# GpSimd waits on a semaphore for VectorE's operation at their shared port, and a planner with other lags orders the kernel

## The chip, the cores and the metric

The kernel runs on one core of one Trainium2 chip. The metric is the device time of one execution in microseconds: 879.89 us for the kernel before, the median of three runs (879.86 to 881.14). The engines are TensorE (PE; PEld is its weight loading), VectorE (DVE), ScalarE (ACT), GpSimd (POOL) and SyncE (SP), whose queue starts nearly all DMA transfers.

## The reference

Three blocks follow one another. Inputs are float32; the weights of the two feed-forward blocks are float64 in the kernel's arrays and are turned into float32 on the chip when they come so.

```python
# attention: 4 batches, 8 heads, 576 positions, 64 per head
scores = q @ k.T / 8
scores = where(scores >= max(scores) - tau, scores, -1e9)
a = exp(scores - max(scores)); a = a / (sum(a) + 1e-9)
x = (a @ v).transpose(0, 2, 1, 3).reshape(2304, 512)
# first feed-forward block, 512 -> 1024 -> 512, with SoLU and a layer norm
h = x @ w_in
s = h * softmax(h)
x = ((s - mean(s)) / sqrt(var(s) + 1e-6) * g_ln) @ w_out
# second feed-forward block, 512 -> 2048 -> 512, with Mish
h = x @ w2_in
out = (h * tanh(log1p(exp(h)))) @ w2_out
```

## The kernel before

The kernel is written as a list of tasks, and a planner puts them in order. Each task names its engine, a duration, the tasks whose results it reads (`deps`), the buffers it takes and those it uses. `Plan.run` (L344) builds the order once with a list scheduler (`forward`, L258) and then issues every task in that order, so each engine's instruction stream is fixed by it. At each step the scheduler picks, for every engine, the ready task with the best rank, and the rank is mainly the task's key: three characters of the table `KEYS` (L19) for each task. A lag is added between a task and one that reads its result (`lag`, L218); a change of TensorE between forms of matmul costs `DRAIN` (L201). Tasks marked `port` (all of GpSimd's, and VectorE's operations that use the port which the two engines share) are planned one after the other. That order at the port is only planned: on the chip each engine starts a task when its own operands are there.

The work has three stages that overlap.

- Attention, to about 410 us. Per pair of heads and block of 128 rows: scores on TensorE (L729 as four-pass float32 products, L737 as products of words split in two), the row maximum on VectorE (L743), the exponential on ScalarE (L744), the threshold on GpSimd (L746, one column), mask and row sum on VectorE (L747), transposes on TensorE (L774 to L779), their copies on ScalarE (L755), and the product with the values (L824). The score tile `st` has two buffers, so L747 on one tile lets a later score product start.
- First feed-forward block, tokens in tiles of 128, from about 30 to 530 us: products with `w_in` (L881), SoLU and layer norm on ScalarE, VectorE and GpSimd (L897 to L911), transposes (L930), products with `w_out` (L951). Float64 weights arrive by DMA and are converted by VectorE (L579 to L587) and GpSimd (L590, L593); each is split into a high and a low word (ScalarE L604, GpSimd L605).
- Second feed-forward block, from about 450 us to the end. Its two products are done with seven block products in place of eight; the sums and differences that this needs are VectorE's and GpSimd's (L640, L969, L1100, L1107, L1171). A product (`product`, L1042) is three matmuls for each chunk of 128: high word by high, low by high, high by low. `ff_in` makes the hidden layer and applies Mish (ScalarE L1103), then splits it into `gh` (L1133) and `gl` (L1135). `ff_out` loads the weight chunk `B7`, splits it (ScalarE L1074, VectorE L1076), and each of its products covers two chunks g of the hidden layer.

In the names, `hoa` and `hob` are the accumulator banks of the last stage, `m` the small tile of row maximum and threshold, `e` the exponentials, `cz` and `cf` the steps of the weight conversion, `ws` the converted weight.

Of the kernel before, what the change touches and what calls it, by code (L numbers as in the profile page):

```python
# [19 lines left out]
    "gb3a+veLPbt8VvljZ9ZCqiUCdfTaZGZm5cfqijBdYnnJga95YPFfc7bC3cXhh1EXXefoyiCrax8X/1g0xb+Dg95dl9a93ifsexPfeQZhedzbcSjf5rcZXeUD"  # L20
    "aoYfREaygewPfUAclGhh7dJ/amSdxtglrdIBcDdbIfdddhDtau3dZibbRV8ecg7bEoirveP3cVbotjX1Wc4UeczdAOhQNexJcubdh/crCZ3MdvWcJJiGnesS"
    "eZvcsXffda3kfMQd3eefOcRWd2ccYJcJ2b9wgMCcNQfkYd5DcwSgYubUFhZBWTfaKDbjnbKGax7dNZat4hppbM8erBes8fZLd3/bgYd1veAxeJpeiheTWdhm"
    "eg6gyvacUfvRcSkdNFawta4DcXMc2gePEhQ6cxUdgDdHVdlkdyBe9zgH4dgXWzxclmcBMdj6cWSdppa/7b3+arAZarYWNesOdInbakZzdd0Fcr4XezV70bkY"
    "XxJayWZcwexWYYyYwkVwPYAIcX5ce4cG/kUtZ4zbc1Yu9d2maukgmxbG9YVNbgEXUTbGnZz/dhydoqclGWoYYoPZcbYmuW41bbpXJXX9WYfAYr6X0Kb89Wu9"
    "cBZWo5ZBdW3GZitY4WacqYWEYfaYmKYSGdxPcVQaqnXi2YGSYZKYIyYtHZw1XsxYAfY0pW9ZUjNZR4XUNXsWXqYZNJedAX2hYIyXl2YfrXqqXuqYTvW61Wo6"
    "ZOxYEGWS1ZRJhzYXlsakAYnDWXjYEfXTfZETWGHbSiXoUX0sTeaZCfXiQXhjXLrWJoYA2YgBW5+aZ1YfPVYrYCIWoBaYjYfnV3hXr1XyrWoKVKBa8MW7fWM9"
    "YnTVilWG5XQmYFZTv3Y8MVEfZ4JXnIW8uWd/Vt3VoiaqMXi2WK8XjlVUJYOaTmhWwGVricBCYZyZnFXxhXmKWEgWanWMST60XRyXZ8ZuoaFMX2+YeuaLqV9p"
    "VokUsoWCPabhXihYfbYLnYc2TdrZCIeEsYkYVmIZDuYdcbIpZF0XiBcUqbvaaOBXOQTTaUKOYgMbyjYoiXb1XTYWSlZXlaZhWZwWt7c4WVKxa+9TP+RtlT1T"
    "WeUZirWRRaBhY+EYdJakSYrBY53bctMfEXldTyMULNYTFSTubTjZkKUqITyBaXdZdpZeIXJWWgVVapT9NS9NWwPTwkYylUAzT4vYV0WEbYTeWxLUH8aAvSef"
    "Za4U9jSVgVYCY4qYV1WP/UxQcb5QbsUjfTycVrGaPFZpbTlPT8qVAkZqvRyhVZ8X2YV8kXD9U1oVXUS5JT/lXdZVC4UCjYiUY4MX3KWDHYvIZk/TIJSqtUg6"  # L30
    "SEVTBVUG5UP+SYtYH3aaYWHjSBwTR3SfMX7JVdoTY5XTVTl5Vf7UPFTilP4vYmuRLNWvjW4wTu/UyLT7ORbPUdvVhBSq+UedRUqU5WSiUTS/VGyWb6VlTTG2"
# [360 lines left out]
def kernel(  # L392
# [30 lines left out]
    CW = 512  # L423
# [839 lines left out]
```

## Time and profile before

| | us |
|---|---|
| median of three runs | 879.89 (879.86 to 881.14) |
| the profiled execution | 878.76 |
| its span, first to last instruction | 876.7 |
| TensorE busy | 850.4 (97%) |
| VectorE busy | 764.1 (87%) |
| ScalarE busy | 614.6 (70%) |
| GpSimd busy | 327.3 (37%) |

The times of single instructions below come from the profiled execution. Matmuls are pipelined and their ends are modelled: a busy TensorE can still be slower than its pace, which is read from the number of matmuls in a stretch. An operation on VectorE or GpSimd that has to wait for the shared port does so inside its own duration, so a long maximum beside a short median is such a wait.

### The profile page before, as it was taken

The page shows a single profiled execution, that of the slowest core. Times are in us where ns is not written, and L with a number is a line of the kernel's source. Part 1 is how long each engine was busy: PE and PEld are TensorE (multiplying, and loading weights), DVE is VectorE, ACT ScalarE, POOL GpSimd, SP SyncE. Part 2 cuts the span into 40 slices and gives each one's busy share as a digit, 9 for nine tenths or more (in the row PEclk, how much of TensorE's full clock was granted, in tenths as well). Part 3 has the DMA queues.
Part 4 walks back from the last instruction along what each step waited for, and adds up shares of the span by engine and source line. Part 5 has one row for each costly group of instructions (what it writes and reads, how often), then busy time and mean ns, then how long its engine had stood idle before and what let it go on. Part 6 is the DMA issues. An engine that isn't in the chain of part 4 may idle for free. (4 is left out here: it accounts for less than half of the span.)

```text
span 876.7 us, 16504 instructions
## 1 busy us (share of the span) xinstructions
PE 850.4 (97%) x5423; PEld 736.1 (84%) x5423; DVE 764.1 (87%) x1638; ACT 614.6 (70%) x1292; POOL 327.3 (37%) x370
## 2 busy tenths in 40 slices
PE   8999999999999999999999999999999999999998
PEld 4556666787787978888888898999999899999998
DVE  6988899889899989999865898998899999878796
ACT  5898988878788878787654776765766555656461
POOL 2677766556675647444222321111122202010000
PEclk8999999999999999999999999999999999999999
DMA  6665444336736384454799499999899869887641
GB/s 225 184 215 190 148 137 144 104 96 201 223 122 186 121 261 156 134 189 132 245 396 306 162 285 310 343 348 332 292 298 336 272 223 307 305 285 252 211 160 72
DMA packets 155573, 195.22 MB, mean 223 GB/s; under 512 B 15312, under 2 KB 112608, under 8 KB 155488
## 3 DMA queue, kind: packets, MB, share of 16 engines
q1 hardware_dynamic: 155344, 194.17, 68.4%
q8 instruction: 43, 0.70, 0.3%
q14 instruction: 42, 0.34, 0.1%
q10 hardware_dynamic: 144, 0.00, 0.0%
HBM read 142.94 MB, written 51.19 MB: 221 GB/s over the span
## 5 line engine op out<-in xcount | busy, mean ns | idle before, releaser
L1047 PE MATMUL hoa<-gh,B 128*128 128x384 f32 x488 | 124.2, 335 | 0.6 <-DVE acc L1171 0.6
L747 DVE SCALAR_TENSOR_TENSOR e<-st,m,e 128x576 f32<-128x576 f32 x139 | 111.4, 813 | 14.9 <-ACT e L744 10.5
L1047 PE MATMUL hoa<-y,A 128*128 128x384 f32 x594 | 117.9, 337 | 3.1 <-ACT gf L1097 2.1
L744 ACT ACTIVATE e<-st,m 128x576 f32<-128x576 f32 x139 | 101.2, 742 | 23.9 <-DVE m L743 23.3
L1107 POOL TENSOR_TENSOR gf<-gf 128x384 f32<-128x384 f32 x24 | 30.7, 1280 | 224.2 <-DVE gf L1107 212.0
L743 DVE TENSOR_REDUCE m<-st 128x1 f32<-128x576 f32 x139 | 102.2, 751 | 11.8 <-PE st L729 6.4
L1047 PEld LDWEIGHTS hoa<-y,A 128*128 128x128 f32 x594 | 103.0, 188 | 6.2 <-ACT gf L1097 3.5
L1133 ACT ACTIVATE gh<-gf 128x384 fp32r<-128x384 f32 x168 | 81.9, 519 | 27.5 <-DVE gf L1107 15.3
L1135 DVE TENSOR_TENSOR gl<-gf,gh 128x384 fp32r<-128x384 f32 x168 | 90.0, 573 | 0.7 <-PE hob L1047 0.7
L774 PE MATMUL p_ta<-ident,e 128*128 128x128 f32 x576 | 84.9, 280 | 4.2 <-ACT ex L755 1.0
L1047 PEld LDWEIGHTS hoa<-gh,B 128*128 128x128 f32 x488 | 87.8, 188 | 1.4 <-DVE acc L1171 1.1
L746 POOL TENSOR_SCALAR m<-m,cs 128x1 f32<-128x1 f32 x144 | 55.6, 388 | 87.1 <-DVE m L743 68.6
L774 PEld LDWEIGHTS p_ta<-ident,e 128*128 128x128 f32 x576 | 66.1, 142 | 24.5 <-ACT ex L755 4.6
L590 POOL TENSOR_TENSOR ws<-cf,cl 128x512 uint32<-128x512 uint32 x32 | 47.0, 1470 | 100.0 <-DMA w2c<-ws 38.3
L951 PE MATMUL p_mo<-LH,W2H 128*128 128x256 f32 x288 | 83.9, 291 | 0.4 <-DVE LL L936 0.4
L951 PE MATMUL p_mo<-LL,W2H 128*128 128x256 f32 x288 | 81.6, 283 | 0.1
L1047 PE MATMUL hoa<-gl,B 128*128 128x384 f32 x244 | 81.6, 334 | 0.0
L951 PE MATMUL p_mo<-LH,W2L 128*128 128x256 f32 x288 | 81.3, 282 | 0.0
L1103 ACT ACTIVATE gf<-gf 128x384 f32<-128x384 f32 x72 | 37.4, 522 | 42.8 <-DVE gf L1100 42.3
L1171 DVE TENSOR_TENSOR acc<-acc,hoa 128x384 f32<-128x384 f32 x106 | 57.0, 548 | 10.8 <-PE hoa L1047 9.6
L881 PE MATMUL p_mo<-W1H,XH 128*128 128x512 f32 x144 | 60.9, 423 | 0.7 <-DVE ln L903 0.6
L729 PE MATMUL st<-Kst,Qhh 64*128 64x320 f32 (+1 forms) x300 | 52.6, 441 | 4.3 <-DVE e L747 2.8
(127 smaller groups left out, 2245.0 us busy)
## 6 DMA issues: line engine op xcount, KB each, us to landing
A<-w2c SPq DMA_DIRECT2D x140, 256.0 KB
y<-yc SPq DMA_DIRECT2D x28, 768.0 KB
w2c<-ws SPq DMA_DIRECT2D x32, 448.0 KB
B<-w2c SPq DMA_DIRECT2D x112, 128.0 KB
cr<-w_in SPq DMA_DIRECT2D x32, 256.0 KB
cr<-w_out SPq DMA_DIRECT2D x32, 256.0 KB
yc<-yh SPq DMA_DIRECT2D x9, 896.0 KB
yc<-ys SPq DMA_DIRECT2D x9, 896.0 KB
```

The costliest lines, as they stand in the source:

```text
L729: TE.matmul(flat()[:, c:c + w], f(qh.tile[a, i * 128:(i + 1) * 128]), f(ks.tile[a, k:k + w]), start=(y == 0), stop=(y == len(heads) - 1))
L743: t = add("DVE", dve(S), lambda: V.tensor_reduce(m.tile[:, 2:3], x(), AX.XY, ALU.max, negate=True), [t], [m], [st])
L744: a = add("ACT", act(S, True) + 0.1, lambda: SC.activation(et(), x(), ACTF.Exp, bias=m.tile[:, 2:3]), [t], [e] if h == 0 else (), [st, m, ...
L746: b = add("POOL", 0.26, lambda: G.tensor_scalar(m.tile[:, 1:2], m.tile[:, 2:3], -1.0, nt8, ALU.mult, ALU.add), [t], use=[m])
L747: t = add("DVE", dve(S) + 0.06, lambda: V.scalar_tensor_tensor(et(), x(), m.tile[:, 1:2], et(), ALU.is_ge, ALU.mult, accum_out=sr.tile[:, ...
L774: TE.transpose(tp.tile[:, k * 128:(k + 1) * 128], e.tile[:, o:o + 128], ident)
L881: TE.matmul(h.tile, l.tile[:, kt], r[:, kt, j * 512:(j + 1) * 512], start=(kt == 0 and x == 0), stop=(kt == KD - 1 and x == 2))
L951: TE.matmul(y.tile[:, :PN], l[:, k, cs], r.tile[:, k], start=(k == 0 and x == 0), stop=(k == KF - 1 and x == 2))
L1047: TE.matmul(x.tile[:, :TH], l, r, start=new and n == 0, stop=stop and n == len(steps) - 1, skip_group_check=True)
L1133: a = add("ACT", act(TH), lambda h=h, x=x: SC.activation(h.tile, full(x), ACTF.Copy), [first], [h], [h, x])
L1135: out[c] = h, l, add(e, cost(TH), lambda h=h, l=l, x=x, eng=eng: eng.tensor_tensor(l.tile, full(x), f(h.tile), ALU.subtract), [a, *deps], ...
L1171: d = add("DVE", dve(TH), lambda: V.tensor_tensor(to(), to(), fr(), ALU.add), deps + [CO.get((v, e, i, t))], use=[ac, x])
```

## The change

Five things change, and with them the order of nearly every engine.

1. After every VectorE task that uses the shared port, the next GpSimd task gets a semaphore wait on it (`add_manual_dep` in `run`). The planner adds 0.2 us (`HAND`) between the two. VectorE's small sum L767 now counts as a user of the port.
2. The lags of the planner are a table by pair of engines (`LAG`), and the cost of a change of form on TensorE is a table (`CHANGE`) in place of 0.24.
3. An operand can be marked `Late`: the planner lets the task start although this operand comes some matmuls later. Tasks with high and low words name each word by itself.
4. `product` takes its terms in turns: with two chunks, one matmul of the first, one of the second, and so on.
5. The table of keys is another, so the order is; some durations in the plan are others.

The diff, cut to its core. Of the 127 lines of the table, before and after, the first stands for all.

```diff
 KEYS = (
-    "gb3a+veLPbt8VvljZ9ZCqiUCdfTaZGZm5cfqijBdYnnJga95YPFfc7bC3cXhh1EXXefoyiCrax8X/1g0xb+Dg95dl9a93ifsexPfeQZhedzbcSjf5rcZXeUD"
+    "io3bPeVUwaR9hdbeQVcd1hnVXPUdbHiNem8zcYDa4yca/gXgczbegzfFuaSHgQ3Y+8d3Fdl8bYnqPtfD0fHfZhWd7Rd51f+9icwYSEhLPfg2dxjb4rfZ0e+3"
...
+class Late:
+    def __init__(self, task, after):
+        self.task, self.after = task, after
...
-    DRAIN = 0.24
+    CHANGE = (0.0, 0.19, 0.135), (0.186, 0.0, 0.1), (0.1, 0.12, 0.0)
+    HAND = 0.2
+    LAG = {"PE": {"ACT": 0.205, "DVE": 0.195}, "ACT": {"ACT": 0.135, "DVE": 0.155, "POOL": 0.19, "PE": 0.165},
+           "DVE": {"DVE": 0.12, "ACT": 0.12, "POOL": 0.2, "PE": 0.16}, "POOL": {"POOL": 0.14, "DVE": 0.1, "PE": 0.12}}
...
     def lag(d, t):
-        if d == t:
-            return 0.0 if t in ("PE", "-") else 0.13
-        return 0.0 if d == "SP" else 0.2 if d == "PE" else 0.27 if t == "PE" else 0.16
+        if d == "SP" or d == t and t in ("PE", "-"):
+            return 0.0
+        return Plan.LAG.get(d, {}).get(t, 0.2 if d == "PE" else 0.16)
...
                     if t.mode != mode:
-                        at = max(at, now + self.DRAIN)
+                        at = max(at, now + self.CHANGE[mode][t.mode])
                 elif t.port:
-                    at = max(at, port)
+                    at = max(at, port, hand if e == "POOL" else 0.0)
...
             if t.port:
                 port = t.end
+                if t.eng == "DVE":
+                    hand = t.end + self.HAND
...
-            t.lags = [(d, self.lag(d.eng, t.eng) if data else None) for d, data in t.need]
+            t.lags = [(d, None if z is None else self.lag(d.eng, t.eng) - z) for d, z in t.need]
...
+            made = self.tc.nc.cur_bb.bb.instructions
+            n = len(made)
             t.fn()
+            if t.port:
+                if t.eng == "DVE":
+                    last = made[-1]
+                elif last is not None:
+                    self.tc.add_manual_dep(made[n], last.name, SYNC, reason="shared port")
+                    last = None
...
-            d = add("DVE", 0.08, lambda: V.tensor_scalar(sums(), sums(), 1.0e-9, None, ALU.add), RX[p][1:], use=[sr])
-            deps = deps + [add("DVE", 0.13, lambda: V.reciprocal(sums(), sums()), [d], use=[sr])]
+            d = add("DVE", 0.08, lambda: V.tensor_scalar(sums(), sums(), 1.0e-9, None, ALU.add), RX[p][1:], use=[sr], port=True)
+            deps = deps + [Late(add("DVE", 0.13, lambda: V.reciprocal(sums(), sums()), [d], use=[sr]), 0.1)]
...
-            steps = [(l, r) for a, b in terms for l, r in zip(a(), b())]
+            steps = [x for y in zip(*(zip(a(), b()) for a, b in terms)) for x in y]
...
-            return product(1, terms, x, new, [Bs[c, g][1] for g in gs] + [GC[v, g][c][2] for g in gs] + deps,
+            return product(1, terms, x, new, [x for n, g in enumerate(gs) for x in (Late(Bs[c, g][1], n * one), Late(Bs[c, g][2], (2 + n) * one), Late(GC[v, g][c][2], n * one), Late(GC[v, g][c][3], (4 + n) * one))] + deps,
```

The products with `w_in` and `w_out` and the value product get `Late` or separate operands in the same manner.

The order of VectorE's instructions at the start of attention, before. `m` is a row maximum, `e` the masked exponentials of the score tile named behind it, `cz` a step of a weight's conversion; L743 to L769 are the same operations under the line numbers of either kernel.

```order
L743 TENSOR_REDUCE m_214<-st_203 128x1
L743 TENSOR_REDUCE m_220<-st_211 128x1
L743 TENSOR_REDUCE m_227<-s3_217 128x1
L747 SCALAR_TENSOR_TENSOR e_222,sr_233<-st_203,m_214,e_222 128x576
L747 SCALAR_TENSOR_TENSOR e_222,sr_233<-st_211,m_220,e_222 128x576
L584 TENSOR_SCALAR cz_241<-cz_241 128x512
L743 TENSOR_REDUCE m_257<-st_243 128x1
L747 SCALAR_TENSOR_TENSOR e_246,sr_233<-s3_217,m_227,e_246 128x576
```

The same place after the change:

```order
L765 TENSOR_REDUCE m_210<-st_202 128x1
L765 TENSOR_REDUCE m_222<-st_212 128x1
L769 SCALAR_TENSOR_TENSOR e_217,sr_226<-st_202,m_210,e_217 128x576
L765 TENSOR_REDUCE m_235<-s3_207 128x1
L769 SCALAR_TENSOR_TENSOR e_217,sr_226<-st_212,m_222,e_217 128x576
L765 TENSOR_REDUCE m_255<-st_237 128x1
L769 SCALAR_TENSOR_TENSOR e_242,sr_226<-s3_207,m_235,e_242 128x576
L765 TENSOR_REDUCE m_268<-st_261 128x1
```

The masked product on the first score tile stands third instead of fourth, and the conversion step is no longer among the first two pairs of tiles.

TensorE's first product of `ff_out`, before: `gh` and `gl` are the high and low half of the hidden layer, `B7` the weight chunk, with a high and a low word, and the bracket names the engine that is waited for.

```order
L1047 MATMUL hob1_7021<-gh_6525,B7_6941 128x384 [waits Activation_49]
L1047 MATMUL hob1_7021<-gh_6525,B7_6941 128x384 [waits DVE_49]
L1047 MATMUL hob1_7021<-gl_6737,B7_6941 128x384
L1047 MATMUL hob1_7021<-gh_6875,B7_6952 128x384 [waits Activation_49]
L1047 MATMUL hob1_7021<-gh_6875,B7_6952 128x384 [waits DVE_49]
L1047 MATMUL hob1_7021<-gl_6987,B7_6952 128x384
```

The same product after the change:

```order
L1070 MATMUL hob1_7003<-gh_6495,B7_6914 128x384
L1070 MATMUL hob1_7003<-gh_6830,B7_6923 128x384
L1070 MATMUL hob1_7003<-gh_6495,B7_6914 128x384 [waits DVE_49]
L1070 MATMUL hob1_7003<-gh_6830,B7_6923 128x384
L1070 MATMUL hob1_7003<-gl_6732,B7_6914 128x384
L1070 MATMUL hob1_7003<-gl_6963,B7_6923 128x384
```

The two chunks alternate; the word that VectorE makes is waited for at the third matmul, where it was the second, and the low half comes fifth and sixth.

GpSimd's stream from the first conversion of a weight to the making of its low word `W1L`, before; `xo` is the attention's output tile, `Qhh` and `Q2` are scaled queries.

```order
L593 TENSOR_TENSOR cf_313<-cf_313,cl_236 128x512 [waits Activation_49]
L689 TENSOR_SCALAR Qhh_262<-Qhh_262,cs_130 128x256 [waits DMAHW2_49,PE_49]
L746 TENSOR_SCALAR m_340<-m_340,cs_130 128x1 [waits DVE_49,Activation_49,Pool_49]
L699 TENSOR_SCALAR Q2_238<-Q2_238,cs_130 128x640 [waits DMAHW0_49]
L746 TENSOR_SCALAR m_357<-m_357,cs_130 128x1 [waits DVE_49,Activation_49,Pool_49]
L689 TENSOR_SCALAR Qhh_327<-Qhh_327,cs_130 128x256 [waits DMAHW5_49,PE_49]
L843 TENSOR_TENSOR xo_332<-xo_332,rx_306 128x256 [waits DMAHW1_49,DMAHW0_49,Activation_49]
L746 TENSOR_SCALAR m_405<-m_405,cs_130 128x1 [waits DVE_49,Pool_49]
L746 TENSOR_SCALAR m_377<-m_377,cs_130 128x1
L689 TENSOR_SCALAR Qhh_371<-Qhh_371,cs_130 128x256 [waits DMAHW3_49,PE_49]
L746 TENSOR_SCALAR m_417<-m_417,cs_130 128x1 [waits DVE_49,Pool_49]
L605 TENSOR_TENSOR W1L_132<-cf_313,W1H_131 128x512 [waits Activation_49]
```

The same stretch after the change:

```order
L615 TENSOR_TENSOR cf_303<-cf_303,cl_311 128x512 [waits Activation_49]
L768 TENSOR_SCALAR m_368<-m_368,cs_130 128x1 [waits DVE_49,Pool_49]
L711 TENSOR_SCALAR Qhh_333<-Qhh_333,cs_130 128x256 [waits DMAHW6_49,PE_49]
L865 TENSOR_TENSOR xo_324<-xo_324,rx_308 128x256 [waits DMAHW7_49,DMAHW0_49,Activation_49]
L627 TENSOR_TENSOR W1L_132<-cf_303,W1H_131 128x512 [waits DVE_49,Activation_49]
L768 TENSOR_SCALAR m_402<-m_402,cs_130 128x1 [waits DVE_49]
L768 TENSOR_SCALAR m_408<-m_408,cs_130 128x1 [waits DVE_49]
L711 TENSOR_SCALAR Qhh_377<-Qhh_377,cs_130 128x256 [waits DMAHW3_49,PE_49]
```

The low word has a wait on VectorE that it did not have, and three operations stand between the conversion and it, where there were ten.

## Rows read from the trace of the kernel before

**Rows 1.** Busy time by stage: span, PE, PEld, DVE, ACT, POOL (instructions); clock, DMA share, GB/s.

```profile
0.00:18.80 18.80, 14.75 (x62) 8.24 (x62) 11.79 (x31) 9.59 (x17) 2.70 (x13) 0.82 0.67 219
18.80:154.00 135.20, 128.80 (x842) 82.72 (x842) 119.78 (x256) 118.11 (x240) 96.82 (x130) 1.00 0.56 172
154.00:308.00 154.00, 150.82 (x1091) 124.27 (x1091) 138.84 (x294) 126.38 (x259) 93.42 (x112) 1.00 0.49 151
308.00:528.00 220.00, 216.28 (x1505) 187.79 (x1504) 185.66 (x402) 157.31 (x307) 85.07 (x83) 1.00 0.71 227
528.00:704.00 176.00, 171.75 (x974) 167.71 (x973) 163.55 (x352) 114.52 (x268) 32.61 (x22) 1.00 0.95 316
704.00:872.90 168.90, 168.00 (x959) 165.38 (x957) 143.98 (x305) 88.73 (x204) 16.63 (x13) 1.00 0.68 227
872.90:876.70 3.80, 0.01 (x1) 0.00 (x0) 0.56 (x1) 0.00 (x0) 0.00 (x0) 0.77 0.37 145
sum 876.70, PE 850.41 PEld 736.11 DVE 764.15 ACT 614.64 POOL 327.26; mean PE 121.49 PEld 105.16 DVE 109.16 ACT 87.81 POOL 46.75
```

**Rows 2.** Waits on TensorE: engine, line waited for, us in total, times, longest.

```profile
PE st L729 <- DVE e L747: 2.8, 4, 1.9
PE hoa L1047 <- ACT gf L1097: 2.1, 3, 1.6
```

**Rows 3.** Busy time in two full stretches of the last stage; columns as above.

```profile
792.00:814.00 22.00, 22.00 (x128) 21.83 (x128) 19.30 (x41) 13.41 (x32) 1.19 (x1) 1.00 0.76 249
814.00:836.00 22.00, 22.00 (x129) 22.00 (x128) 15.95 (x32) 10.57 (x22) 2.40 (x2) 1.00 0.71 226
```

**Rows 4.** All engines in order of time at the start: start, us, instruction, [idle before].

```profile
1.19 4.18 PE L527 MATMUL p_ta<-warm 128*128 128x512 bf16 x11 [1.19 <-DVE warm L524]
...
1.66 1.37 SPq L687 DMA_DIRECT2D Qhh<-qq  x3
...
6.00 0.35 DVE L689 TENSOR_SCALAR Qhh<-Qhh,cs 128x256 f32<-128x256 f32 x1 [1.33 <-DMA Qhh<-qq]
...
7.27 0.76 DVE L743 TENSOR_REDUCE m<-st 128x1 f32<-128x576 f32 x1 [0.25 <-PE st L729]
...
7.94 0.75 DVE L743 TENSOR_REDUCE m<-s 128x1 f32<-128x576 f32 x1
...
8.61 0.81 DVE L747 SCALAR_TENSOR_TENSOR e<-st,m,e 128x576 f32<-128x576 f32 x1
...
9.57 0.77 PE L729 MATMUL st<-Kst,Qhh 64*128 64x320 f32 x4 [1.92 <-DVE e L747]
...
11.30 0.43 DVE L584 TENSOR_SCALAR cz<-cz 128x512 f32<-128x512 f32 x1 [1.14 <-ACT cz L582]
...
11.64 0.75 DVE L743 TENSOR_REDUCE m<-st 128x1 f32<-128x576 f32 x1
```

**Rows 5.** All engines in order of time, entry to the second feed-forward block.

```profile
528.65 0.43 DVE L579 TENSOR_SCALAR cz<-cr 128x512 uint32<-128x512 uint32 x1 [1.54 <-DMA cr<-w_in]
...
531.93 0.53 ACT L1103 ACTIVATE gf<-gf 128x384 f32<-128x384 f32 x1 [3.00 <-DVE gf L1100]
...
534.24 1.32 PE L1047 MATMUL hoa<-y,A 128*128 128x384 f32 x6 [1.56 <-ACT gf L1097]
...
536.24 0.44 PE L1047 MATMUL hob<-gh,B 128*128 128x384 f32 x1 [0.50 <-DVE B L1076]
```

**Rows 6.** Port users by line: count, duration ns min/median/max, first and last start us.

```profile
L640 DVE TENSOR_TENSOR ws<-ws x128: 227/285/1653, 178.4 to 731.4; 128x128 f32<-128x128 f32 x128
...
L579 DVE TENSOR_SCALAR cz<-cr x32: 412/428/1793, 162.2 to 723.3; 128x512 uint32<-128x512 uint32 x32
...
L746 POOL TENSOR_SCALAR m<-m,cs x144: 255/266/1321, 7.1 to 406.4; 128x1 f32<-128x1 f32 x144
```

**Rows 7.** TensorE in order of time at two changes between forms of matmul.

```profile
60.36 0.81 PE L729 MATMUL st<-Kst,Qhh 64*128 64x256 f32 x4 [0.16 <-PE p_ta L824]
...
88.78 0.81 PE L729 MATMUL st<-Kst,Qhh 64*128 64x256 f32 x4 [0.22 <-issue]
```

More of the change, by code (lines that the diff above doesn't have):

```diff
@@ L209, in add @@
         t.new = list(new)
-        t.need = [(d, True) for d in deps if d is not None] + [(d, False) for d in order if d is not None]
+        t.need = [(d.task, d.after) if isinstance(d, Late) else (d, 0.0) for d in deps if d is not None]
+        t.need += [(d, None) for d in order if d is not None]
         for x in t.new:
@@ L292, in put @@
         def put(b, t, open_, stale):
-            nonlocal port, dma, table, mode
+            nonlocal port, hand, dma, table, mode
             t.begin, t.end = b, b + t.dur
@@ L364, in run @@
                 if x.k:
[L365 removed]
+                    t.need.append((b.slots[x.k - 1].taker, None))
                 if b not in self.rings:
@@ L574, in convert @@
             hw = lambda: cr.tile[:, :, 1]
-            t2 = add("ACT", act(CW), lambda: SC.activation(cl.tile, cr.tile[:, :, 0], ACTF.Copy, scale=2.0 ** -29),
+            t2 = add("ACT", 0.56, lambda: SC.activation(cl.tile, cr.tile[:, :, 0], ACTF.Copy, scale=2.0 ** -29),
                      t_f, [cl], [cr])
@@ L581, in convert @@
             else:
-                t1 = add("ACT", act(CW), lambda: SC.activation(f(cz.tile), f(hw()), ACTF.Abs), t_f, [cz], [cr], table="exp")
+                t1 = add("ACT", 0.56, lambda: SC.activation(f(cz.tile), f(hw()), ACTF.Abs), t_f, [cz], [cr], table="exp")
             t3 = chain("DVE", [
@@ L832, in pv @@
         for ks in (range(0, 2), range(2, KT), range(KT, QT)):
-            t = add("PE", pe(len(ks), w, 4) + 0.015, lambda ks=ks: go(ks), [d for y in [*x, u] for d in y[1:]] + [vt] if t is None else [],
+            t = add("PE", pe(len(ks), w, 4) + 0.015, lambda ks=ks: go(ks), [d for y in x for d in y[1:]] + [vt] if t is None else u[1:] if KT in ks else [],
                     [acc] + [xo] * (not xo.taker) if t is None else (), [acc, v] + slots, order=[t or xo.taker], mode=2)
-        EVT[p].append(add("ACT", act(w, True) + 0.05, lambda: SC.activation(xo.tile[:, cs], acc.tile[:, :w], ACTF.Copy),
+        EVT[p].append(add("ACT", act(w, True), lambda: SC.activation(xo.tile[:, cs], acc.tile[:, :w], ACTF.Copy),
                           [t], (), [acc, xo]))
@@ L876, in moe_h @@
         so, (xh, xl) = SO[t][0], XSL[t]
-        h, last_t = b_two.new(), None
+        h, last_t, one = b_two.new(), None, pe(1, 512)
         def go(kt):
@@ L884, in moe_h @@
         for kt in range(KD):
-            last_t = add("PE", pe(3, 512) + 0.02, lambda kt=kt: go(kt), XSP[t] + [W1T[kt, c] for c in range(j * 512, j * 512 + 512, CW)],
+            last_t = add("PE", pe(3, 512) + 0.02, lambda kt=kt: go(kt), [XSP[t][0], Late(XSP[t][1], 2 * one)] + [x for c in range(j * 512, j * 512 + 512, CW) for x in (W1T[kt, c][0], Late(W1T[kt, c][1], one))],
                          [h] + [so] * (j == 0) if kt == 0 else (), [h, xh, xl], order=[last_t or (so.taker if j else None)])
@@ L1134, in ff_in @@
             e, cost, eng = ("POOL", gps, G) if c in LOWP else ("DVE", dve, V)
-            out[c] = h, l, add(e, cost(TH), lambda h=h, l=l, x=x, eng=eng: eng.tensor_tensor(l.tile, full(x), f(h.tile), ALU.subtract), [a, *deps], [l], [h, l, x], port=True)
+            out[c] = h, l, a, add(e, cost(TH), lambda h=h, l=l, x=x, eng=eng: eng.tensor_tensor(l.tile, full(x), f(h.tile), ALU.subtract), [a, *deps], [l], [h, l, x], port=True)
         GC[z, g] = out
```

293 lines of the change are left out of this document (147 added, 146 removed).

## The prediction

> **What bounds the kernel now.** I read the busy time by stage first, because a mean over the whole span hides what a stage is limited by. In it TensorE is busy for 850.4 of 876.7 us [rows 1]. Its idle time is 4.05 us in the first 18.8 us, 6.40 up to 154, 3.18 up to 308, 3.72 up to 528, 4.25 up to 704, 0.90 up to 872.9 and 3.8 us behind its last matmul: 26.3 us together. VectorE stands next, at 89% between 18.8 and 154 and 93% between 528 and 704. So the end is set by TensorE's work plus the pauses that late operands force on it, and nothing in this change adds or removes a matmul. Only pauses can go.
>
> Second, the busy figure is not the pace. In two full stretches of the last stage 257 matmuls of 128x384 take 44 us, 0.1712 us each [rows 3]. At that pace the 974 matmuls between 528 and 704 need 166.7 us of 176.0, so 9.3 us are lost there, twice what idle time shows; the 959 up to 872.9 need 164.2 of 168.9, so 4.7 are lost. The reader is to see that a stall hides its first tenths under the modelled end of the matmul before it.
>
> Third, who is late: in the attention half it is mostly VectorE's masked product (2.8 us in 4 waits), in the feed-forward half ScalarE's copy (2.1 us in 3) [rows 2]. The longest case of each is followed below.
>
> **The change part by part.** The same 4943 matmuls, 1476 VectorE, 1252 ScalarE and 366 GpSimd operations are issued, counted in both orders; so every term is an idle interval or a wait.
>
> *The start.* VectorE's first masked product, which frees the score tile for TensorE's fourth score product, stands behind three reductions now and behind two in the new order. The second reduction ran from 7.27, and the third began at 7.94 and pushed the product to 8.61; TensorE idled 1.92 us for it and began at 9.57 [rows 4]. With two reductions ahead the product can begin near 8.02, 0.6 us sooner. Then a weight conversion on VectorE waited 1.14 us for ScalarE and took 0.34 to the next start, in front of the reduction at 11.64 [rows 4]; in the new order it stands after that pair of heads is done. That is up to 1.48 us for the chain of VectorE. The start cannot fall below the warm-up matmuls, which run from 1.19 for 4.18 us in both [rows 4]. In SP's queue the second pair of operands changes places: the query goes from fourth to second, its key from second to fifth. Three query issues take 1.37 us [rows 4], 0.46 each, so a fifth place lands some 0.46 after the fourth, which was scaled at 6.00; a product of the first head goes ahead of it and covers this. I take -1.0 us, bounds -1.5 and 0: what a start gains is kept only if later stages wait on the same chain.
>
> *Attention and mixture, 18.8 to 528.* All keys that rank the instructions are new, and lags from ScalarE and VectorE to TensorE are planned 0.1 us shorter. I cannot follow each move, so I bound the sum: from below all 13.3 us of idle there (6.40, 3.18 and 3.72) gone, from above the same 13.3 lost again, since new orders also make new waits. Between ends so far apart I go by the nearest row: the stage from 154 to 308 lives with 2.1% idle. The stage before it at that share would take 128.80/0.979 = 131.5 instead of 135.2 us. I take -3.7.
>
> *The feed-forward half, 528 to 872.9.* The longest stall, 1.56 us at 534.24, has a chain: VectorE waits 1.54 us for a weight from DRAM, ScalarE 3.00 us for VectorE's sum, TensorE for ScalarE's copy [rows 5]. The transfer model is not touched, so such a late landing can come again. But the products of the second block change inside: the two chunks alternate, so the low word of a weight, for which TensorE idled 0.50 us at 536.24 [rows 5], is wanted by the third matmul instead of the second, 0.171 us later, and the low half of the activation by the fifth instead of the third, 0.34 us later. The planner also stops holding a whole product until its last operand is there. Bounds: -14.0 (9.3 and 4.7) and +4.7 (the better half's loss once more). The nearest row is again the better half: at its loss of 2.8% the stretch to 704 would take 171.5 us. I take -4.5.
>
> *Changes of matmul form.* TensorE goes between the three forms (four-pass scores, value product, everything else) 118 times in the old order and 130 in the new, counted there. Two such changes cost 0.16 and 0.22 us of idle [rows 7]; twelve more give +1.9 to +2.6, from below 0 where the engine would have waited anyway. I take +1.9.
>
> *GpSimd's wait.* In the old order 217 of GpSimd's 375 rows already wait on VectorE, in the new one 233. What both do without the wait: VectorE's small sums take 285 ns, but 1653 at worst, its first conversion step 428 and 1793, and GpSimd's one-column operation 266 and 1321 [rows 6]; the difference at the worst is one whole operation of the other engine. The Trainium skill, SBUF — State Buffer, section Who interferes with whom, says that the shared pair is an exclusive lock, that whichever engine issues first has it for the whole instruction, and that the other blocks fully. Those maxima agree. By that rule a semaphore removes no port time, it only says who stands still, and this part of the sum would be nought. The wait's price: 16 more waits of up to one conversion step, 0.428 us, are 6.8 us of GpSimd; it idles 38.4 us between 18.8 and 154 [rows 1], which hides most. Behind a held one-column operation stands VectorE's masked product. Bounds -3 (VectorE's worst case, 1.37 us, met twice less on the path) and +6.8; I take +1.0, near the cover.
>
> Sum: -1.0 -3.7 -4.5 +1.9 +1.0 = -6.3 us on a span of 876.7. The profiled execution took 878.76, 2.06 around its span; the median of the three runs shown is 879.89, 1.13 above it. So 879.89 - 6.3 = 873.6 us.
>
> **Rivals.** *Deeper (863 to 870):* a plan whose lags hold is kept by the engines, and half of all that is lost goes: of 2.86 at the start (4.05 less the 1.19 ahead of the warm-up [rows 4]), 13.3 in the middle and 14.0 at the end, half is 15.1; less 2.9 for the changes of form and the wait this gives 867.7. For it: VectorE at 93% would lose its collisions. Against: late transfers stay.
>
> *Nothing to measure:* the new order trades stalls one for one; only the start (-1.0) and the forms (+1.9) are left, 880.8. For it: the attention stages are already 95 to 98% busy. That GpSimd's wait does next to nothing, since 217 rows waited before, belongs here.
>
> *Slower:* GpSimd becomes the bound between 18.8 and 154. It has 130 operations and 38.4 us of slack there [rows 1], 0.295 us for each. If the semaphore makes each wait longer than that on average, the rest goes onto the path through the one-column operation, VectorE's product and the score tile. At 0.36 us (between 0.295 and 0.428) the excess is 8.4; with -4.5, -1.0 and +1.9, and no gain in that stage, +4.8 or 884.7. For it: GpSimd is at 72% there. Against: only some of the rows wait anew.
>
> **How the numbers follow.** Chances: forecast 0.50 (own range 870 to 877.5), deeper 0.18, no change 0.15, slower 0.17. Measurements of this kernel tell 0.2% from no change, 878.1 to 881.7 here. Forecast and deeper lie below it: faster 0.68; same 0.15; slower 0.17. The range 866 to 883 leaves out the deepest cases and the upper half of the slow ones.
>
> **What would show it.** Right: TensorE idle between 18.8 and 154 near 3 us, the fourth score product begun before 9.2 us, the loss between 528 and 704 near 5 us, and VectorE's small sums without maxima above 1 us. Wrong: GpSimd above 85% busy or waiting on VectorE between 18.8 and 154 with TensorE idle longer there; a new stall over 1.5 us behind a transfer at the entry to the feed-forward blocks; or the same idle time in other places.

## The result, and the profile after

The changed kernel takes 871.72 us (median of 4 runs, 871.35 to 873.1), against 880.51 us for the kernel before (median of 4 runs, 879.86 to 881.57). The ratio is 0.990, with a 95% interval of 0.989 to 0.992: 8.8 us faster. The forecast was 873.6. The profiled execution has a span of 870.2 us; 876.7 less the forecast sum of 6.3 was 870.4. The number is right. Most of its terms are not, and the experiments show it. The kernel before was measured again beside each group of experiments: 879.65 us (17 runs), 879.16 (21) and 879.86 (18); the ratios below are to the group's own.

The stages of the changed kernel, columns as in [rows 1]: span, then busy time and instructions of PE, PEld, DVE, ACT and POOL.

```profile
0.00:18.80 18.80, 14.75 (x78) 7.91 (x78) 12.56 (x32) 10.55 (x18) 3.68 (x13) 1.00 0.75 229
18.80:154.00 135.20, 128.22 (x841) 84.43 (x839) 114.72 (x255) 117.08 (x240) 84.62 (x125) 1.00 0.55 169
154.00:308.00 154.00, 151.02 (x1095) 122.65 (x1095) 131.40 (x282) 129.13 (x263) 85.91 (x113) 1.00 0.49 147
308.00:528.00 220.00, 216.45 (x1504) 190.60 (x1501) 179.87 (x407) 154.47 (x306) 79.64 (x84) 1.00 0.71 227
528.00:704.00 176.00, 174.26 (x1000) 172.93 (x999) 163.84 (x373) 121.82 (x282) 26.43 (x23) 1.00 0.97 322
704.00:866.40 162.40, 160.30 (x917) 158.35 (x915) 135.61 (x293) 81.82 (x190) 13.78 (x13) 1.00 0.71 235
...
sum 870.20, PE 845.04 PEld 736.88 DVE 738.55 ACT 614.87 POOL 294.06; mean PE 120.72 PEld 105.27 DVE 105.51 ACT 87.84 POOL 42.01
```

Against [rows 1], TensorE's idle time is 6.98 us where it was 6.40 up to 154, 2.98 after 3.18 up to 308, 3.55 after 3.72 up to 528: in idle time the attention half has hardly changed. Between 528 and 704 it is 1.74 where it was 4.25, and 1000 matmuls ran where there were 974. At 0.1712 us each [rows 3] these are 26 x 0.1712 = 4.5 us. Behind 704 the loss at that pace is 5.4 us where it was 4.7. The other surprise stands in the last line. VectorE runs the same 1638 instructions in 738.55 us instead of 764.15, GpSimd the same 370 in 294.06 instead of 327.26. An operation that stands at the shared port does so inside its duration, so 25.6 and 33.2 us of standing there are gone. The lines behind that, VectorE's small sums and GpSimd's one-column operation after the change (duration min/median/max in ns), answer to [rows 6]:

```profile
L662 DVE TENSOR_TENSOR ws<-ws x128: 273/284/1014, 194.5 to 719.3; 128x128 f32<-128x128 f32 x128
```

```profile
L768 POOL TENSOR_SCALAR m<-m,cs x144: 255/265/806, 8.1 to 397.9; 128x1 f32<-128x1 f32 x144
```

The medians are within 1 ns of those before (284 and 265 ns); the maxima fell from 1653 to 1014 and from 1321 to 806, so the forecast's sign of no maximum above 1 us is met but for 14 ns.

TensorE at the start after the change:

```profile
5.99 1.19 PE L751 MATMUL st<-Kst,Qhh 64*128 64x256 f32 x4
...
9.85 0.77 PE L751 MATMUL st<-Kst,Qhh 64*128 64x320 f32 x4 [1.69 <-DVE e L769]
```

The fourth score product begins at 9.85, not before 9.2 as forecast and later than the 9.57 of [rows 4], because the first one begins only at 5.99: its key now is the third transfer in SP's queue.

One row of the start was not read in the forecast: the clock granted to TensorE. Before, it is 0.82 on average up to 18.8 us [rows 1]. It is 1.00 up to 10 us and 0.50, the lower of its two levels (1.2 of 2.4 GHz), from 12 to 18; TensorE had been busy for 0.43 us between 8 and 10:

```profile
8.00:10.00 2.00, 0.43 (x4) 0.33 (x4) 2.00 (x5) 0.74 (x1) 0.53 (x2) 1.00 0.95 350
12.00:18.00 6.00, 5.36 (x23) 4.30 (x24) 5.10 (x13) 4.45 (x10) 0.98 (x3) 0.50 0.42 155
```

After the change it is 1.00, and 78 matmuls ran up to 18.8 us where 62 had, in the same 14.75 us of busy time. These 16 are most of the 18 that the changed kernel is ahead at 528. No run ties the time to it: of the 17 runs of the kernel before (876.87 to 883.63 us) four had a mean clock of 1.0 and took 877.56 to 880.78 us, and the old order with the wait on whole tiles (below) has 0.91 and 62 matmuls there and the lowest median of all.

### The profile page after: what moved, and what is told of

Same layout as the page of the kernel before. It is cut to its first block, busy times and chain, and to the rows that moved or that the text cites. A ratio compares the mean times of both kernels' runs of the same rounds, so it can differ in the third digit from the quotient of the medians.

```text
span 870.2 us, 16492 instructions
## 1 busy us (share of the span) xinstructions
PE 845.0 (97%) x5423; PEld 736.9 (85%) x5423; DVE 738.5 (85%) x1638; ACT 614.9 (71%) x1292; POOL 294.1 (34%) x370
## 4 chain that ended last, share of the span: by engine, by line
PE 83%; DVE 5%; DMA 4%; ACT 4%; issue 2%; POOL 2%; SPq 0%; POOLq 0%; ACTq 0%; DVEq 0%
PE hoa L1070 28%; PE p_mo L903 11%; PE hob L1070 9%; PE p_ta L846 9%; PE p_mo L973 9%; PE p_ta L796 6%; PE st L759 5%; PE st L751 4%; DMA B<-w2c 2%; PE p_mo L952 1%; DVE m L765 1%; DVE e L769 1%; PE p_ta L799 1%; ACT e L766 1%; DMA A<-w2c 1%
## 5 line engine op out<-in xcount | busy, mean ns | idle before, releaser
L1070 PE MATMUL hoa<-y,A 128*128 128x384 f32 x678 | 132.3, 336 | 1.8 <-ACT gf L1120 0.9
L769 DVE SCALAR_TENSOR_TENSOR e<-st,m,e 128x576 f32<-128x576 f32 x139 | 111.5, 814 | 18.0 <-POOL m L768 8.6
L1070 PEld LDWEIGHTS hoa<-y,A 128*128 128x128 f32 x678 | 118.1, 188 | 3.1 <-ACT gf L1120 1.5
L1130 POOL TENSOR_TENSOR gf<-gf 128x384 f32<-128x384 f32 x24 | 24.4, 1017 | 232.4 <-DVE gf L1130 108.8
L1070 PE MATMUL hoa<-gh,B 128*128 128x384 f32 x464 | 99.4, 335 | 0.6 <-DVE acc L1194 0.6
L1070 PEld LDWEIGHTS hoa<-gh,B 128*128 128x128 f32 x464 | 82.0, 188 | 1.3 <-DVE acc L1194 1.1
L768 POOL TENSOR_SCALAR m<-m,cs 128x1 f32<-128x1 f32 x144 | 39.2, 275 | 119.8 <-DVE m L765 37.5
L612 POOL TENSOR_TENSOR ws<-cf,cl 128x512 uint32<-128x512 uint32 x32 | 41.3, 1289 | 103.5 <-DVE gl L1158 16.4
L1194 DVE TENSOR_TENSOR acc<-acc,hoa 128x384 f32<-128x384 f32 x104 | 56.1, 550 | 8.0 <-PE hoa L1070 6.4
L1070 PE MATMUL hoa<-gl,B 128*128 128x384 f32 x232 | 59.2, 335 | 0.0
L973 PEld LDWEIGHTS p_mo<-LH,W2H 128*128 128x128 f32 x288 | 54.9, 191 | 3.9 <-issue 2.2
```

Source lines behind the costliest of these rows:

```text
L769: t = add("DVE", dve(S) + 0.06, lambda: V.scalar_tensor_tensor(et(), x(), m.tile[:, 1:2], et(), ALU.is_ge, ALU.mult, accum_out=sr.tile[:, ...
L973: TE.matmul(y.tile[:, :PN], l[:, k, cs], r.tile[:, k], start=(k == 0 and x == 0), stop=(k == KF - 1 and x == 2))
L1070: TE.matmul(x.tile[:, :TH], l, r, start=new and n == 0, stop=stop and n == len(steps) - 1, skip_group_check=True)
L1194: d = add("DVE", dve(TH), lambda: V.tensor_tensor(to(), to(), fr(), ALU.add), deps + [CO.get((v, e, i, t))], use=[ac, x])
```

## The experiments

Two theories stood against each other at first. A: the new order makes the gain, and the semaphore only says who stands still; this is the prediction's. B: the gain comes from keeping the planned order at the port.

**The semaphore taken from the changed kernel.** The order of every engine stays.

```diff
-                    self.tc.add_manual_dep(made[n], last.name, SYNC, reason="shared port")
+                    pass
```

> The changed kernel without the semaphore waits at the port; the order of every engine is unchanged. Theory A (the new order as a whole makes the gain, and the semaphore only says who stands still): 871.7 us, within 871 to 873.5, although VectorE's small sums go back from a mean of 304 ns towards the 381 of before. Theory B (what counts is that the planned order at the port is kept): at least half of the 8.8 us is given back, 876 to 881, and TensorE's idle time between 528 and 704 us rises from 1.74 towards 4.25 us.

Measured: 892.88 us, ratio to the kernel before 1.016 (1.013 to 1.018). A falls. The new order alone is 13 us slower than the old one, and the loss is beyond what B expected too. The stretch of the last stage and the whole span of this run, columns as above:

```profile
528.00:704.00 176.00, 169.47 (x971) 164.37 (x970) 165.33 (x345) 113.80 (x264) 31.86 (x21) 1.00 0.94 311
0.00:891.10 891.10, 853.81 (x5423) 739.07 (x5423) 772.08 (x1638) 615.08 (x1292) 333.85 (x370) 1.00 0.68 219
```

TensorE is idle 6.53 us between 528 and 704, VectorE is busy 772.08 us and GpSimd 333.85. What a GpSimd operation meets that has no wait is seen in order of time (start, us, engine, line):

```profile
687.68 4.41 POOL L1130 TENSOR_TENSOR gf<-gf 128x384 f32<-128x384 f32 x1 [8.08 <-DVE gf L1130]
687.72 0.55 DVE L1130 TENSOR_TENSOR gf<-gf 128x384 f32<-128x384 f32 x1
...
688.19 0.75 DVE L1099 TENSOR_TENSOR B<-B 128x256 fp32r<-128x256 f32 x2
...
688.86 0.55 DVE L1130 TENSOR_TENSOR gf<-gf 128x384 f32<-128x384 f32 x1
...
689.33 1.08 DVE L644 TENSOR_TENSOR ws<-ws,wh 128x896 fp32r<-128x896 f32 x1
...
690.33 0.41 DVE L1099 TENSOR_TENSOR B<-B 128x256 fp32r<-128x256 f32 x1
690.67 0.55 DVE L1158 TENSOR_TENSOR gl<-gf,gh 128x384 fp32r<-128x384 f32 x1
691.13 1.47 DVE L1194 TENSOR_TENSOR acc<-acc,hoa 128x384 f32<-128x384 f32 x3
```

The difference on GpSimd, about 1.02 us where it is alone, became ready in a run of VectorE's operations and took 4.41 us, while VectorE's took their usual time. VectorE left no gap. GpSimd's operation ended at 692.09, 0.96 us after VectorE had turned to the sums L1194, which read one operand from an accumulator bank: it was served beside these, and not before. TensorE's waits on VectorE sum to 19 us in this run, where the changed kernel has 11.

**The semaphore alone on the kernel before.** Old keys, old lags, old order.

```diff
...
             t.fn()
+            if t.port:
+                if t.eng == "DVE":
+                    last = made[-1]
+                elif last is not None:
+                    self.tc.add_manual_dep(made[n], last.name, SYNC, reason="shared port")
+                    last = None
```

> The kernel before with only the semaphore waits added. Theory A: 880.5, between 879 and 883 us, since the old order was not planned for them. Theory B: 874 to 877 us. In both the mean of VectorE's small sums falls from 381 to near 300 ns and that of GpSimd's one-column operation from 388 to near 275.

Measured: 871.76 us, ratio 0.991 (0.989 to 0.993). That is the whole gain, and 2 us more than B's range had. The two means went to 314 and 303 ns, the second not as far as expected. The last stage and the span of this run:

```profile
528.00:704.00 176.00, 174.65 (x999) 172.66 (x998) 163.77 (x367) 119.41 (x280) 25.07 (x22) 1.00 0.96 323
0.00:869.40 869.40, 846.41 (x5423) 734.80 (x5423) 748.45 (x1638) 613.20 (x1292) 299.55 (x370) 1.00 0.69 225
```

999 matmuls between 528 and 704 and 1.35 us of idle time, as in the changed kernel, without any of its other four parts.

**The turns, taken out of the changed kernel (the diff) and put alone into the old one (the same line the other way round).**

```diff
-            steps = [x for y in zip(*(zip(a(), b()) for a, b in terms)) for x in y]
+            steps = [(l, r) for a, b in terms for l, r in zip(a(), b())]
```

> The changed kernel with the three matmuls of one chunk before those of the next, as before; order of tasks and semaphores unchanged. If the turns matter (theory C), the plan's later operands are now wanted up to two matmuls too early, 0.34 us each time: 873 to 876 us, with waits of TensorE on VectorE's low words in the last stage. Theory A without C: 871.7, within 0.7.

> The kernel before with only the terms of a product taken in turns. Theory C: the low words are wanted one or two matmuls later, 879 to 880 us, and the wait of 0.50 us on VectorE's low word at 536 us is shorter by 0.17. Against it: the second chunk's high words are wanted 0.34 us earlier, which makes new waits and gives 880.5 to 882.

Measured: 871.59 us without the turns (ratio 0.991, 0.989 to 0.993), and 879.53 us with the turns alone (ratio 1.000, 0.998 to 1.002). The turns are worth nothing that can be measured, in either order. The step itself does what was said of it: TensorE's wait for the low word of a weight in the old order is 0.3 us where it was 0.50 [rows 5]. Without the turns the new order has the same density between 528 and 704 (waits on TensorE in the first, busy times in the second):

```profile
PE hob L1047 <- DVE B L1076: 0.3, 1, 0.3
```

```profile
528.00:704.00 176.00, 174.81 (x1001) 173.12 (x1000) 164.41 (x374) 122.89 (x282) 26.44 (x23) 1.00 0.96 322
```

The count of one stretch is to be read with the stretch ahead of it: the turns alone have 991 matmuls between 528 and 704, 17 more than before, but 17 fewer between 440 and 528.

**Which operations.** The wait on the old order only for GpSimd's whole-tile operations, and only for its one-column operation. The diff is against the semaphore alone.

```diff
-                elif last is not None:
+                elif last is not None and t.dur > 0.3:    # in the other kernel: t.dur < 0.3
```

> The kernel before with the semaphore wait only for GpSimd's whole-tile operations (planned at over 0.3 us); its one-column operation L746 stays free. The wait alone gave 871.8 us on the old order. Theory B1 (the harm is that a whole-tile operation takes the port ahead of VectorE's planned one and holds it for 1.3 us, or comes in the middle of a run of VectorE's and stands until it ends): most of the gain, 871 to 874.5. Theory B2 (the harm is the threshold, the one-column operation, standing at the port while VectorE's masked product waits for it): 878 to 880.5.

> The kernel before with the semaphore wait only for GpSimd's one-column operation L746 (planned at 0.26 us). Theory B1: 878 to 880.5, with the small sums of VectorE still near 381 ns. Theory B2: 871 to 874.5, and GpSimd's one-column operation from a mean of 388 to near 300 ns.

Measured: 870.26 us (ratio 0.990, 0.988 to 0.992) for the whole tiles and 878.41 us (1.000, 0.998 to 1.001) for the one column. B1 holds, without a run that parts its two cases from each other, and the wait for the one-column operation, on which the prediction's slower rival rested, does not matter. Yet both cut the standing at the port; with the one column alone VectorE's small sums fell to a mean of 337 ns, where B1 expected 381. The run with the wait for the one column alone:

```profile
0.00:440.00 440.00, 426.35 (x2953) 325.54 (x2954) 385.87 (x839) 354.42 (x715) 242.77 (x319) 1.00 0.55 172
440.00:873.70 433.70, 423.64 (x2471) 409.55 (x2469) 372.21 (x801) 259.80 (x578) 71.95 (x52) 1.00 0.82 275
sum 873.70, PE 849.98 PEld 735.09 DVE 758.07 ACT 614.22 POOL 314.72; mean PE 424.99 PEld 367.54 DVE 379.04 ACT 307.11 POOL 157.36
```

GpSimd needs 314.72 us, 12.5 less than before and close to the 310.51 that the whole tiles leave; VectorE needs 758.07, 6.1 less, where the whole tiles save it 16.6 (747.51, the sum further below). The time stays. So the sum of the standing is not what counts, and it matters which operation stands. One case from the kernel before, in the last stage:

```profile
695.16 1.30 POOL L590 TENSOR_TENSOR ws<-cf,cl 128x512 uint32<-128x512 uint32 x1 [8.04 <-DVE cf L587]
...
695.42 1.99 DVE L622 TENSOR_TENSOR ws<-ws,wh 128x896 fp32r<-128x896 f32 x1
...
697.33 1.47 DVE L1171 TENSOR_TENSOR acc<-acc,hoa 128x384 f32<-128x384 f32 x3
...
698.86 0.62 PE L1047 MATMUL hoa<-gh,B 128*128 128x384 f32 x2 [0.58 <-DVE acc L1171]
```

GpSimd's conversion took the port 0.26 us ahead of VectorE's subtraction on a whole weight tile, which then lasted 1.99 us. Behind it in VectorE's stream stood three sums into the output, L1171, and TensorE idled 0.58 us for the last of them, which ended at 698.80. With 1.08 us for the subtraction, as below, it would have ended 0.91 us sooner, ahead of TensorE's need at 698.28 (an estimate from these rows). The same place with the wait on whole tiles:

```profile
689.30 1.08 DVE L632 TENSOR_TENSOR ws<-ws,wh 128x896 fp32r<-128x896 f32 x1
...
690.30 1.48 DVE L1181 TENSOR_TENSOR acc<-acc,hoa 128x384 f32<-128x384 f32 x3
...
690.47 1.29 POOL L600 TENSOR_TENSOR ws<-cf,cl 128x512 uint32<-128x512 uint32 x1 [4.86 <-DVE ws L632]
```

The subtraction takes 1.08 us, the sums follow, and GpSimd starts behind it. The second face of it is the difference L1107, which both engines do (L1117 under the numbers of this experiment), first before, then with the wait:

```profile
L1107 DVE TENSOR_TENSOR gf<-gf x72: 544/557/1391, 515.2 to 860.9; 128x384 f32<-128x384 f32 x72
L1107 POOL TENSOR_TENSOR gf<-gf x24: 1013/1332/1701, 515.9 to 856.1; 128x384 f32<-128x384 f32 x24
```

```profile
L1117 DVE TENSOR_TENSOR gf<-gf x72: 544/552/1365, 512.7 to 852.6; 128x384 f32<-128x384 f32 x72
L1117 POOL TENSOR_TENSOR gf<-gf x24: 1007/1017/1396, 514.3 to 847.7; 128x384 f32<-128x384 f32 x24
```

GpSimd's median falls from 1332 to 1017 ns. VectorE's maximum stays: it is not made to wait for GpSimd's planned operation.

The case is not a single one. These are all of TensorE's waits on VectorE in the products of the last stage before (waits over 0.15 us are listed):

```profile
PE hoa L1047 <- DVE acc L1171: 0.6, 1, 0.6
PE hoa L1047 <- DVE gf L1100: 0.6, 1, 0.6
...
PE hob L1047 <- DVE B L1076: 0.5, 1, 0.5
...
PE hob L1047 <- DVE acc L1171: 0.2, 1, 0.2
```

They make 1.9 us. With the wait on the one column they are 2.2 us and with all waits 0.7; with the wait on whole tiles none is left, and none with its late half alone (next), where the early half leaves 1.6. In the new order they are 5.3 us without the wait and 2.5 with it. No run shows which of the whole-tile operations matters most, or what a delay of GpSimd would do that is not tied to VectorE.

**Where.** The wait for whole tiles only behind 440 us of the plan, and only up to there. The diff is against the wait on whole tiles.

```diff
-                elif last is not None and t.dur > 0.3:
+                elif last is not None and t.dur > 0.3 and t.begin > 440.0:    # in the other kernel: <= 440.0
```

> The kernel before with the wait for GpSimd's whole-tile operations only where the plan puts them behind 440 us (some 50 operations: sums of the last stage, layer norm, late weights). The same wait on all of them gave 870.3 us against 879.2. Theory B1 late (the harm is in the last stage, where every VectorE operation uses the port and TensorE waits for its results): 871.5 to 874.5. Theory B1 early (the harm is with the 300 operations of attention): 877 to 880.

> The kernel before with the wait for GpSimd's whole-tile operations only where the plan puts them up to 440 us. Theory B1 late: 876 to 878.5 (the part of the gain that TensorE has at 440 us when all have the wait, 14 matmuls or some 2 us). Theory B1 early: 870 to 873. The two halves should add up to the whole, 8.9 us, if they do not touch each other.

Measured: 874.84 us (ratio 0.994, 0.992 to 0.996) with the late half and 876.67 us (0.996, 0.995 to 0.998) with the early one. Each is a part, and 0.0061 + 0.0038 make 0.0099 of the 0.0101 that both have together. The late operations are some 50 of 370 and make over half of it. One thing in the late theory is not so: the sums L1100 and L1171 of the last stage are not marked as users of the port, and beside GpSimd's conversion at 690.47 above three of them (L1181 there) took 1.48 us, as before. Busy times up to 440 us and in two stages, for the early half alone, for the late half alone, and then up to 440 us for both:

```profile
0.00:440.00 440.00, 427.22 (x2963) 327.96 (x2964) 386.91 (x843) 356.30 (x717) 251.05 (x319) 1.00 0.56 175
...
154.00:308.00 154.00, 152.36 (x1111) 126.62 (x1109) 136.48 (x301) 127.59 (x262) 92.59 (x114) 1.00 0.51 155
...
528.00:704.00 176.00, 173.06 (x980) 169.04 (x980) 164.91 (x357) 116.61 (x273) 32.71 (x22) 1.00 0.95 317
```

```profile
0.00:440.00 440.00, 425.05 (x2942) 324.48 (x2943) 391.55 (x834) 354.58 (x714) 254.94 (x318) 1.00 0.55 171
...
154.00:308.00 154.00, 150.38 (x1088) 123.82 (x1087) 138.88 (x294) 125.79 (x256) 94.04 (x113) 1.00 0.49 150
...
528.00:704.00 176.00, 174.08 (x1000) 171.83 (x999) 161.19 (x360) 116.89 (x274) 25.09 (x22) 1.00 0.97 322
```

```profile
0.00:440.00 440.00, 425.37 (x2962) 327.43 (x2963) 385.85 (x843) 356.31 (x717) 250.97 (x319) 1.00 0.55 175
...
sum 868.30, PE 845.16 PEld 736.12 DVE 747.51 ACT 613.28 POOL 310.51; mean PE 422.58 PEld 368.06 DVE 373.75 ACT 306.64 POOL 155.25
```

At 440 us the early half has 2963 matmuls done and both have 2962, the late half 2942 as against 2948 before. The early gain is made between 154 and 308, 1111 matmuls where there were 1091 [rows 1], and the late one between 528 and 704, 1000 where there were 974. Since the two add up, what is won early is kept to the end.

**The wait in both directions, on the changed kernel.**

```diff
                 if t.eng == "DVE":
+                    if back is not None:
+                        self.tc.add_manual_dep(made[n], back.name, SYNC, reason="shared port")
+                        back = None
                     last = made[-1]
-                elif last is not None:
+                else:
+                    back = made[-1]
+                if t.eng == "POOL" and last is not None:
```

> The changed kernel with the wait in both directions: VectorE's next port operation also waits for GpSimd's planned one. If what counts is that the planned order at the port is kept (theory B in its full form): 866 to 871 us, since VectorE still stands at the port in 26 cases for 15.6 us. If only GpSimd's side counts, because VectorE must never stand idle: 872 to 880, VectorE now waits with nothing at the port whenever GpSimd is late.

Measured: 873.94 us, ratio 0.994 (0.993 to 0.996) against the change's 0.990 (0.989 to 0.992): slower by 0.4%. In the same group the change with only its first key moved (next) took 870.65 us. The trace shows no standing at the port any more, and the time is not better. The span's busy times, then VectorE's small sums and GpSimd's one-column operation (duration min/median/max in ns):

```profile
0.00:870.60 870.60, 844.88 (x5423) 736.36 (x5423) 724.41 (x1638) 615.97 (x1292) 291.34 (x370) 1.00 0.69 224
```

```profile
L667 DVE TENSOR_TENSOR ws<-ws x128: 274/284/295, 194.8 to 721.4; 128x128 f32<-128x128 f32 x128
...
L773 POOL TENSOR_SCALAR m<-m,cs x144: 257/267/283, 7.1 to 399.3; 128x1 f32<-128x1 f32 x144
```

VectorE's busy time is 724.41 us, 14 less than after the change. But its idle waits on GpSimd sum to some 40 us, where the changed kernel has 11. So B in its full form falls as well: what pays is that GpSimd gives way to VectorE, not that both keep the plan.

**The first key in front, on the changed kernel (the diff); the wait on whole tiles, on the changed kernel (`t.dur > 0.3` as above); both.**

```diff
+        sp = [t for t in order if t.eng == "SP"]
+        order.remove(sp[2])
+        order.insert(order.index(sp[0]), sp[2])
```

> The changed kernel with one transfer moved: the first key goes to the front of SP's queue, as in the kernel before; the order is otherwise the same. The first score product should begin at 5.3 us in place of 5.99. If a start is kept to the end: 871.0, 0.7 faster. If later waits take it back: 871.7, within 0.5.

> The changed kernel with the wait only for GpSimd's whole-tile operations. If the one-column operation needs no wait (B1), 870.0 to 872 us, the same as the change or up to 1.5 faster as on the old order (871.8 to 870.3). If the new order, planned with 0.2 us behind VectorE, needs the wait there too: 873 to 880.

> The changed kernel with the wait only for whole-tile operations and the first key at the front of SP's queue. If both small gains hold and add up, 869 to 870.3 us; if they are noise, 871.7.

Measured: 870.65 us (ratio 0.991, 0.989 to 0.993), 871.88 us (0.990, 0.988 to 0.993) and 871.54 us (0.991, 0.988 to 0.994). None is told apart from the change. The start did move by about a microsecond; TensorE's first and fourth score products in the run with the key in front:

```profile
5.05 0.81 PE L754 MATMUL st<-Kst,Qhh 64*128 64x256 f32 x4
...
8.52 0.77 PE L754 MATMUL st<-Kst,Qhh 64*128 64x320 f32 x4 [1.69 <-DVE e L772]
```

The first begins at 5.05 and the fourth at 8.52, 0.94 and 1.33 us before the changed kernel's; no run shows that it is kept to the end.

The old order with the wait on whole tiles, 870.26 us, has the lowest median of all, but its interval and the change's overlap: the two can't be told apart, and it needs a few lines of the change.

## Why the prediction was right and wrong

The time and the sign held; 871.7 lies in the forecast's own range of 870 to 877.5. That is luck: the sum credits -9.2 us to the new order, which by itself gains nothing that a run shows, and +1.0 us to the wait, which makes the gain. By its steps:

- *GpSimd's wait, +1.0 us.* This is the step that failed. On the old order it measures 871.76 - 879.65 = -7.9 us and on the new one 871.7 - 892.9 = -21.2. The step priced the wait by the 16 rows that wait anew on VectorE. The count misses the rest: by the edit, a row that already waited for an earlier task of VectorE now waits for the last one at the port. For the gain the step went by the rule of the Trainium skill, SBUF — State Buffer, section Who interferes with whom, that the port goes whole to whoever issues first. The rule agrees with the 1.99 us above. The inference that the prediction drew, that a semaphore is then worth nought, does not hold for the path: of TensorE's waits before, about 10 us in 18 cases are on VectorE and 1.2 us in two on GpSimd, so it matters who stands. [Rows 6] had the cue, maxima of 1.65 us on VectorE's small sums, and the step bounded its gain at 3 us as if two such cases were on the path.
- *Attention and mixture, -3.7 us, from the new order.* Not shown: TensorE's idle time from 18.8 to 528 is 13.51 us (6.98, 2.98 and 3.55) where it was 13.30, and the new order without the wait is 13 us slower. In the old order what is won up to 440 us is the wait's (2963 matmuls with its early half against 2948), and it is made between 154 and 308, the stage that the step took as the good one.
- *The feed-forward half, -4.5 us.* The place is right, and nearly the size: 26 matmuls more up to 704, 4.5 us, and 0.7 us more lost behind it. The cause is wrong: the turns measure nothing, and the old order with the wait has 999 of the 1000 matmuls there.
- *The start, -1.0 us.* The masked product stands behind two reductions as said, but the step costed the key's fifth place for the second head pair and not the third place of the first key; the first product came 0.69 us later. The warm-up matmuls, put at 4.18 us in both, took 4.87. TensorE's idle time up to 18.8 us is 4.05 us in both; the step did not see the clock of 0.82 in its own row. Moving that key changed the start and not the time that can be measured.
- *Changes of form, +1.9 us.* Not isolated by a run.
- *The rivals.* That the wait does next to nothing, since 217 rows waited before, fails with the step above. The slower rival named the right wait with the wrong sign: GpSimd is busy 84.62 us between 18.8 and 154 where it was 96.82, since waiting at the semaphore is not standing at the port.
- *The signs.* The loss between 528 and 704 came out near 5 us (176.0 less 1000 x 0.1712 is 4.8). TensorE's idle time between 18.8 and 154, forecast near 3 us, is 6.98, and the fourth score product came later, not sooner. For the attention half the sign of being wrong holds: the same idle time in other places.

What stays open: why the new order without the wait is 13 us slower than the old one without it. It was planned with a gap of 0.2 us for the wait, and with shorter lags, but neither was changed alone. With the wait, the old order and the new one can't be told apart (871.76 and 871.72 us), so what keys, lags and `Late` are worth is open too.

## What to carry to other kernels

Where two engines share a port, look for operations whose maximum is their median plus one whole operation of the other engine, and ask which of the two stands in front of the bound engine: make the other one wait for it by a semaphore; here it paid in that direction only. Test such a wait on the old schedule before crediting a new one; here a reordering of everything, 13 us slower by itself, hid behind it. Less standing is not the measure: the wait on the one-column operations took 18.6 us of it from the two engines and gave nothing.

## What the runs showed of the hardware

A GpSimd operation that is ready in a run of VectorE's port operations was not served between them: 4.41 us for one of about 1.02 while six rows of VectorE's passed at their usual durations. It was served once VectorE turned to sums with an operand in an accumulator bank. Two conversions of about 1.29 us did the same: 3.64 us from 732.16 in the run without the semaphore and 3.73 us from 665.32 before, ended 1.23 and 1.25 us after such a sum began. And removing the standing at the port by waits in both directions was slower by about 0.4% than leaving VectorE free.
